# A gated linear-attention kernel with a fused MoE: the decay's row moved to the ACT queue and used one step later, another order of the first units, and the x transposes in another PSUM bank

## The chip, the cores and the metric

The kernel runs on one core of a Trainium2 chip. TensorE (PE) does matmuls and transposes, VectorE (DVE), ScalarE (ACT) and GpSimd (POOL) the elementwise work, and SyncE (SP) issues DMAs. An engine takes its instructions in order, so one that waits holds up all that stand behind it on that engine. The metric is device time in microseconds of one execution; several are made and the median is given. The profile comes from one more execution; its span runs from the first to the last instruction.

## The reference

Two stages are computed in float32. The first is a recurrence over 768 tokens for each of 4 batches and 8 heads of width 48, with a decay `w` per token and channel; the second is a two-matrix "maxout" MLP over the tokens.

```python
for t in range(S):                        # S = 768
    cur = einsum('bhd,bhe->bhde', u * kt, vt)
    y[:, :, t] = einsum('bhd,bhde->bhe', rt, state + cur)
    state = wt[:, :, :, None] * state + einsum('bhd,bhe->bhde', kt, vt)
x = y.transpose(0, 2, 1, 3).reshape(3072, 384)
out = maximum(x @ w1, x @ w2) @ w_out     # w1, w2: 384 x 1024, w_out: 1024 x 384
```

## The kernel before

The recurrence is done in chunks of 128 tokens. A **unit** is one chunk of two batches, so there are 12 units: unit n is chunk n // 2 of batches 0 and 1 (n even) or 2 and 3 (n odd). The 128 partitions hold 64 token pairs of each of the two batches. The state of the recurrence passes from unit n to unit n + 2, through `S_f` (float32) and `S_b` (bfloat16).

Each unit goes through three stages, and one **step** works on three units at once: stage A on unit n, stage T on unit n - 1, stage M on unit n - 2.

- Stage A: log of the decays (`logw`, done for the next unit), their prefix sum by a matmul with a triangular matrix (`cumsum`, into PSUM bank `ex`, line 195), exponentials (`exps`, lines 206 and 208), and the scaled r and k (`scale_rk`, lines 228 and 229). The sum of the whole chunk's logs, one row of `mz` per batch, is what the state decays by. It stands along one partition and is wanted down the partitions, so `exps` writes it to DRAM (`row`, line 212, two DMAs) and `decay_load` fetches it back into `WL` (line 221, two DMAs, element by element). Both are issued on SP.
- Stage T: transposes of the scaled r and k (`transp`, line 236, bank `tr`), the new state term (`kv`, into `T_f`), the scores (`scores`, lines 288 and 291), y (`y_inter`, `y_intra`), its cast to bfloat16 (line 328) and its transposes (`xt`, line 335, bank `tr` too, copied out by ACT at line 337). `decay_exp` (line 246, on ACT) turns `WL` into the decay factor, and `decay` (lines 274 and 277, on POOL) makes the next state of it, at the start of the following step.
- Stage M: the MLP. maximum(a, b) is taken as half of (a + b) + |a - b|: `gate` multiplies x by w1 - w2 and takes the absolute value (lines 347 and 351), `outp` adds the two products (lines 359 and 362), copies the result to `osb` (line 365) and stores it (line 368). The store's destination is seen as 2 x 64 x 384 (the two tokens of a pair, the pairs, the columns).

`weights` makes w1 - w2, w1 + w2 and the product (w1 + w2) w_out / 2 once (lines 142 to 156); it stands between stage T of unit 1 and the first stage M.

The order of work on every engine is the order in which it is written; no planner moves it. The three weights and the loads of units 0 to 2 are issued on SP ahead of all; in step n, SP gets the fetch of unit n - 1's decay, the eight load DMAs of unit n + 2 (line 77, 196,608 bytes each, w before k, r and v), unit n's row, and unit n - 2's two stores (196,608 bytes each). The load tiles have four buffers. Waits between engines are put in by the framework. It gives the DMAs, whichever queue they are on, eight completion counters in turn, and a DMA is issued only when the earlier one with its counter has landed.

Of the kernel before, what the change touches and what calls it, by code (L numbers as in the profile page):

```python
# [8 lines left out]
F32 = mybir.dt.float32  # L9
BF16 = mybir.dt.bfloat16  # L10
AF = mybir.ActivationFunctionType
# [23 lines left out]
def _body(tc, r, k, v, w, u, moe_w1, moe_w2, moe_w_out, out):  # L35
    nc = tc.nc
    B, H, S, D = r.shape
    P = 128
    C = 128
    Q = C // 2  # L40
    NC = S // C
    HD = H * D
    d_ff = moe_w1.shape[1]
    KO = HD // P
    FO = d_ff // P
    NP = H // 2
    DP = 64
    NU = NC * B // 2
# [15 lines left out]
    def unit(n):  # L64
        return n // 2, (n % 2) * 2
# [5 lines left out]
    def load(n):  # L71
        c, b0 = unit(n)
        d = {}
        for name, src in (("w", w), ("k", k), ("r", r), ("v", v)):
            t = ldp.tile([P, H, 2, D], F32, tag="l" + name, name="l" + name)
            for b in range(2):
                nc.sync.dma_start(  # L77
                    out=t[b * Q:(b + 1) * Q].rearrange("p h i d -> p h (i d)"),
                    in_=src[b0 + b, :, c * C:(c + 1) * C, :].rearrange(
                        "h (p i) d -> p h (i d)", i=2))  # L80
            d[name] = t
        L[n] = d
# [36 lines left out]
    for i in range(NRK):  # L119
        t = const.tile([P, 2, 2, H, DP], BF16, name=f"rkn{i}")  # L120
        nc.vector.memset(t, 0.0)
        rkn_b.append(t)

    S_f = [const.tile([P, 2, NP, D], F32, name=f"Sf{g}") for g in range(2)]
    T_f = [const.tile([P, 2, NP, D], F32, name=f"Tf{g}") for g in range(2)]
# [14 lines left out]
    def weights():  # L140
        for ko in range(KO):
            nc.vector.tensor_sub(wd_sb[:, ko, :], w1f[:, ko, :], w2f[:, ko, :])
            nc.vector.tensor_add(ws_sb[:, ko, :], w1f[:, ko, :], w2f[:, ko, :])
        nc.scalar.mul(wo_sb, wof, 0.5)
        for ko in range(KO):
            tp = pt_([P, FO, P], BF16, "tr")
            for fo in range(FO):
                nc.tensor.transpose(tp[:, fo, :], ws_sb[:, ko, fo * P:(fo + 1) * P], ident)
            nc.vector.tensor_copy(
                wsT_sb.rearrange("p f (k c) -> p k f c", k=KO)[:, ko, :, :], tp)  # L150
        for ko in range(KO):
            wc_p = pt_([P, HD], F32, "go", 2)
            for fo in range(FO):
                nc.tensor.matmul(wc_p, wsT_sb[:, fo, ko * P:(ko + 1) * P],  # L154
                                 wo_sb[:, fo, :], start=(fo == 0), stop=(fo == FO - 1))
            nc.scalar.copy(wc_sb[:, ko, :], wc_p)
# [7 lines left out]
    def logw(n):  # L164
        s = U[n] = {}
        s["lw"] = lw = wt_([P, H, 2, D], F32, "lw")
        nc.scalar.activation(lw, L[n]["w"], AF.Ln)  # L167
        s["lp"] = lp = wt_([P, H, D], F32, "lp")
        nc.gpsimd.tensor_add(lp, lw[:, :, 0, :], lw[:, :, 1, :])  # L169
# [21 lines left out]
    def cumsum(n):  # L191
        s = U[n]
        lw, lp = s["lw"], s["lp"]
        ex = pt_([P, HD], F32, "ex")
        nc.tensor.matmul(ex, tri2, lp.rearrange("p h d -> p (h d)"))  # L195
        s["A"] = A = wt_([P, 2, H, D], F32, "A")
        s["mz"] = mz = wt_([P, 2, HD], F32, "mz")
        exh = ex.rearrange("p (h d) -> p h d", h=H)
        nc.scalar.activation(A[:, 0], exh, AF.Exp)  # L199
        nc.vector.tensor_add(mz[:, 0].rearrange("p (h d) -> p h d", h=H), exh, lw[:, :, 0, :])  # L200
        nc.vector.tensor_add(mz[:, 1], ex, lp.rearrange("p h d -> p (h d)"))

    def exps(n):
        s = U[n]
        mz = s["mz"]
        nc.scalar.activation(s["A"][:, 1].rearrange("p h d -> p (h d)"), mz[:, 0], AF.Exp)
        s["iA"] = iA = wt_([P, 2, H, D], F32, "iA", 1)
        nc.scalar.activation(iA.rearrange("p i h d -> p i (h d)"), mz, AF.Exp, scale=-1.0)
        row = drp.tile([2, HD], F32, tag="row", name="row")
        for b in range(2):  # L210
            e = (b + 1) * Q
            nc.sync.dma_start(out=row[b:b + 1, :], in_=mz[e - 1:e, 1, :])
        s["row"] = row

    def decay_load(n):
        s = U[n]
        row = s["row"]
        s["WL"] = wl = WL[n % 2]
        rowv = row.rearrange("b (p r d) -> r d (b p)", r=2, d=D)
        for par in range(2):  # L220
            nc.sync.dma_start(
                out=wl[par * DP:par * DP + D, :, :].rearrange("d b p -> d (b p)"),
                in_=rowv[par])

    def scale_rk(n):
        s = U[n]
# [4 lines left out]
    def transp(n, x):  # L231
        s = U[n]
        tp = pt_([P, NP, 2, 2, Q], BF16, "tr")
        for i in range(2):
            for p in range(NP):
                nc.tensor.transpose(  # L236
                    tp[:, p, :, i, :],
                    s["rkn"][:, x, i, 2 * p:2 * p + 2, :].rearrange("s r d -> s (r d)"), ident)
# [4 lines left out]
    def decay_exp(n):  # L243
        s = U[n]
        s["Wt"] = wt = wt_([P, 2, NP, 1], F32, "Wt")
        nc.scalar.activation(wt.rearrange("p b q o -> p b (q o)"), s["WL"], AF.Exp)  # L246
# [82 lines left out]

    def xt(n):  # L330
        s = U[n]
        tp = pt_([P, KO, 2, P], BF16, "tr")
        for b in range(2):
            for ko in range(KO):
                nc.tensor.transpose(tp[:, ko, b, :], s["x"][:, b, ko * P:(ko + 1) * P], ident)  # L335
        s["xT"] = xT = wt_([P, KO, 2, P], BF16, "xT")
        nc.scalar.copy(xT, tp)  # L337
# [16 lines left out]
    def outp(n, b):  # L354
        c, b0 = unit(n)
        s = U[n]
        o = pt_([P, HD], F32, "go", 2)
        for ko in range(KO):
            nc.tensor.matmul(o, s["xT"][:, ko, b, :], wc_sb[:, ko, :],  # L359
                             start=(ko == 0), stop=False)  # L360
        for fo in range(FO):
            nc.tensor.matmul(o, s["gT"][:, fo, b, :], wo_sb[:, fo, :],  # L362
                             start=False, stop=(fo == FO - 1))
        osb = wt_([P, HD], F32, "osb", 6)
        nc.scalar.copy(osb, o)  # L365
        tok = (b0 + b) * S + c * C
        dst = out[tok:tok + C, :].rearrange("(q i) n -> i q n", i=2)
        nc.sync.dma_start(out=dst, in_=osb)


    def step(a, t, m):

        A, T, M = a is not None, t is not None, m is not None
        if T and t >= 1: decay(t - 1)
        if T: transp(t, 0)
        if A: cumsum(a)
        if M: gate(m, 0)
        if T: transp(t, 1)
        if A: exps(a)
        if A: bonus_mul(a)  # L380
        if M: gate(m, 1)
        if T: kv(t)
        if T: scores(t, 0)
        if A and a + 1 < NU: logw(a + 1)
        if M: gate(m, 2)
        if M: gate(m, 3)
        if T: decay_exp(t)
        if T: scores(t, 1)
        if T: y_inter(t)
        if A: scale_rk(a)  # L390
        if A: bonus_sum(a)
        if M: outp(m, 0)
        if T: y_intra(t)
        if M: outp(m, 1)
        if T: xt(t)
# [52 lines left out]
```

## Time and profile before

| | us |
|---|---|
| median of three runs | 240.19 (237.9 to 241.53) |
| the profiled execution | 237.25 |
| its span | 235.5 |
| PE busy | 157.3 (67%) |
| DVE busy | 106.7 (45%) |
| ACT busy | 91.2 (39%) |
| POOL busy | 105.7 (45%) |
| DMA engines (mean of 16) busy with the one hardware queue | 57.1% |

The page gives busy time of each engine, the chain of work that ended last (each piece followed back to what released it), and groups of instructions with what ended the idle time before them. A row of the chain reads: start, length, what. A row of the timeline reads: start, length, engine, line, operation, output <- inputs, count, and in brackets the idle time before it and what ended it. A row of waits reads: who waited for whom, then the total, the number and the longest of the waits. "SPq" is SP's queue: the time in which it issues a DMA. DMA share is the mean busy share of the core's 16 DMA engines; it can be above 1 where packets overlap.

### The profile page before, as it was taken

The numbers are of one execution on the slowest core, as the hardware profiler recorded it, in microseconds if no ns is written. First come the engines' busy times: TensorE is split into PE (matmuls) and PEld (weight loads), VectorE is DVE, ScalarE is ACT, GpSimd is POOL, SyncE is SP. The second block draws the span as 40 slices with busy tenths as digits, with TensorE's granted clock in tenths as the row PEclk, the third lists the DMA queues.
The fourth block names the chain that finished last, engine by engine and source line by source line (L and its number), as shares of the span: only waits on it lengthen the run. The fifth ranks groups of instructions, "written<-read, shape, count | busy, mean of one in ns | idle before, by whom it ended". The sixth has DMA issues, their size and how long they took to land.

```text
span 235.5 us, 5089 instructions
## 1 busy us (share of the span) xinstructions
PE 157.3 (67%) x2104; PEld 105.8 (45%) x2104; DVE 106.7 (45%) x135; ACT 91.2 (39%) x161; POOL 105.7 (45%) x116
## 2 busy tenths in 40 slices
PE   0316300553889979759889499893997939979820
PEld 0114200432555747437565375662665626665610
DVE  5336600189243837516666056570584905642000
ACT  3313001207164747047271463624536345453510
POOL 7299004910008759284393743947429476200000
PEclk9999999999999999968999779998599997999985
DMA  6999995959200386492674936939459201010110
GB/s 135 214 212 372 388 223 99 208 90 203 37 1 10 76 172 112 106 196 57 163 147 104 187 73 154 156 84 187 88 134 180 54 23 46 22 44 26 44 48 38
DMA packets 65463, 28.91 MB, mean 123 GB/s; under 512 B 60424, under 2 KB 64672, under 8 KB 65440
## 3 DMA queue, kind: packets, MB, share of 16 engines
q1 hardware_dynamic: 65440, 28.59, 57.1%
q8 instruction: 16, 0.26, 0.4%
q14 instruction: 7, 0.06, 0.1%
HBM read 23.83 MB, written 4.76 MB: 121 GB/s over the span
## 4 chain that ended last, share of the span: by engine, by line
PE 28%; DMA 21%; SPq 18%; DVE 12%; ACT 7%; issue 6%; POOL 3%; DVEq 0%; ACTq 0%
SPq L77 15%; DMA WL<-row 13%; DMA row<-mz 8%; PE go L347 6%; PE go L362 4%; PE tr L236 4%; PE ex L195 3%; ACT xT L337 2%; DVE M L291 2%; POOL vd L186 2%; PE go L154 2%; PE sc L288 2%; PE go L359 2%; DVE rkn L228 2%; PE tr L335 2%
## 5 line engine op out<-in xcount | busy, mean ns | idle before, releaser
L347 PE MATMUL go<-xT,wd_sb 128*128 128x256 bf16 x288 | 41.0, 290 | 2.0 <-ACT xT L337 0.9
L241 DVE COPY rT<-tr 128x1024 bf16<-128x1024 bf16 x12 | 8.3, 691 | 65.5 <-PE tr L236 65.5
L362 PE MATMUL go<-wo_sb,gT 128*128 128x384 bf16 x192 | 35.1, 326 | 0.0
L347 PEld LDWEIGHTS <-wd_sb 128*128 128x128 bf16 x288 | 28.8, 104 | 12.7 <-issue 7.1
L186 POOL TENSOR_TENSOR vd<-lv,dg 128x768 bf16<-128x768 f32 x12 | 17.7, 1474 | 36.9 <-DVE dg L184 36.8
L291 DVE TENSOR_TENSOR M<-sc,mask 128x1024 bf16<-128x1024 f32 x24 | 29.4, 1223 | 8.6 <-PE sc L288 8.6
L169 POOL TENSOR_TENSOR lp<-lw 128x384 f32<-128x384 f32 x12 | 12.0, 997 | 46.6 <-ACT lw L167 46.4
L351 ACT ACTIVATE gT<-go 128x512 bf16<-128x512 f32 x48 | 27.8, 593 | 9.7 <-PE go L347 9.2
L335 PE MATMUL tr<-ident,x 128*128 128x128 bf16 x72 | 7.3, 251 | 32.3 <-ACT x L328 32.3
L236 PE MATMUL tr<-ident,rkn 128*128 128x128 bf16 x192 | 19.3, 261 | 12.5 <-ACT xT L337 8.9
L246 ACT ACTIVATE Wt<-WL 128x8 f32<-128x8 f32 x12 | 2.5, 209 | 60.7 <-DMA WL<-row 60.7
L362 PEld LDWEIGHTS <-gT 128*128 128x128 bf16 x192 | 18.7, 98 | 12.5
L236 PEld LDWEIGHTS <-rkn 128*128 128x128 bf16 x192 | 16.6, 119 | 16.8 <-issue 12.0
L195 PE MATMUL ex<-lp,tri 128*128 128x384 f32 x24 | 14.8, 709 | 12.2 <-POOL lp L169 12.2
L176 POOL TENSOR_TENSOR rku<-lr,lk 128x768 f32<-128x768 f32 x12 | 22.4, 1866 | 0.0
L177 POOL TENSOR_TENSOR rku<-rku,u_b 128x768 f32<-128x768 f32 x12 | 21.8, 1815 | 0.9
L335 PEld LDWEIGHTS <-x 128*128 128x128 bf16 x72 | 5.1, 111 | 35.9 <-ACT x L328 35.6
L167 ACT ACTIVATE lw<-lw 128x768 f32<-128x768 f32 x12 | 10.0, 837 | 19.3 <-DMA lw<-in_w_dram 19.3
L359 PE MATMUL go<-wc_sb,xT 128*128 128x384 bf16 x72 | 15.7, 328 | 0.4 <-ACT gT L351 0.4
L200 DVE TENSOR_TENSOR mz<-ex,lw 128x384 f32<-128x384 f32 x12 | 6.7, 558 | 19.5 <-ACT A L199 19.5
L199 ACT ACTIVATE A<-ex 128x384 f32<-128x384 f32 x12 | 5.9, 490 | 23.9 <-PE ex L195 23.9
L365 ACT COPY osb<-go 128x384 f32<-128x384 f32 x24 | 11.4, 475 | 8.0 <-PE go L362 8.0
(55 smaller groups left out, 225.1 us busy)
## 6 DMA issues: line engine op xcount, KB each, us to landing
lw<-in_w_dram SPq DMA_DIRECT2D x24, 192.0 KB
lk<-in_k_dram SPq DMA_DIRECT2D x24, 192.0 KB
lr<-in_r_dram SPq DMA_DIRECT2D x24, 192.0 KB
lv<-in_v_dram SPq DMA_DIRECT2D x24, 192.0 KB
out_dram<-osb SPq DMA_DIRECT2D x24, 192.0 KB
w1f<-in_moe_w_dram SPq DMA_DIRECT2D x1, 1536.0 KB
w2f<-in_moe_w_dram SPq DMA_DIRECT2D x1, 1536.0 KB
wof<-in_moe_w_out_dram SPq DMA_DIRECT2D x1, 1536.0 KB
```

The costliest lines, as they stand in the source:

```text
L77: nc.sync.dma_start(out=t[b * Q:(b + 1) * Q].rearrange("p h i d -> p h (i d)"), in_=src[b0 + b, :, c * C:(c + 1) * C, :].rearrange("h (p i ...
L176: nc.gpsimd.tensor_mul(rku, L[n]["r"], L[n]["k"])
L177: nc.gpsimd.tensor_mul(byi(rku), byi(rku), u_b.rearrange("p (h d) -> p h d", h=H).unsqueeze(1).to_broadcast([P, 2, H, D]))
L186: nc.gpsimd.tensor_mul(byi_inv(vd), L[n]["v"], dg.to_broadcast([P, H, 2, D]))
L195: nc.tensor.matmul(ex, tri2, lp.rearrange("p h d -> p (h d)"))
L236: nc.tensor.transpose(tp[:, p, :, i, :], s["rkn"][:, x, i, 2 * p:2 * p + 2, :].rearrange("s r d -> s (r d)"), ident)
L291: nc.vector.tensor_mul(M.rearrange("s e p t -> s (e p) t"), sc.rearrange("s e p t -> s (e p) t"), mask[:, i].rearrange("s i q -> s (i q)") ...
L335: nc.tensor.transpose(tp[:, ko, b, :], s["x"][:, b, ko * P:(ko + 1) * P], ident)
L347: nc.tensor.matmul(g[:, f, :], wd_sb[:, ko, fo * P:(fo + 1) * P], s["xT"][:, ko].rearrange("p j t -> p (j t)"), start=(f == 0 and ko == 0) ...
L351: nc.scalar.activation(s["gT"][:, 2 * j:2 * j + 2].rearrange("p f j t -> p f (j t)"), g, AF.Abs)
L359: nc.tensor.matmul(o, s["xT"][:, ko, b, :], wc_sb[:, ko, :], start=(ko == 0), stop=False)
L362: nc.tensor.matmul(o, s["gT"][:, fo, b, :], wo_sb[:, fo, :], start=False, stop=(fo == FO - 1))
```

## The change

The diff does four things.

1. The chunk's row and its fetch are issued on ACT instead of SP. `mz` becomes two fixed tiles with the heads padded from 48 to 64 columns (cleared once by POOL), so the row is stored by one DMA and fetched by one DMA of 128 x 8 elements. The fetch stands at the start of stage T's step. For the last chunk (units 10 and 11), whose state nobody reads, row, fetch and exponential are left out.
2. `decay_exp` and `decay` of unit t - 1 stand in the middle of the step in which unit t is in stage T: the exponential comes one step after its fetch, and not in the same step.
3. The x transposes write bank `ex` instead of `tr`, and the output copies have four buffers instead of six.
4. The first steps are written out: in the step of unit 1 the log of unit 2 is left out; it is done after `weights`. The loads of units 3 and 4 stand after step 0 and after `weights`.

```diff
+    MZ = [const.tile([P, 2, H, DP], F32, name=f"mz{i}") for i in range(2)]
+    for t in MZ:
+        nc.gpsimd.memset(t, 0.0)
...
-        s["mz"] = mz = wt_([P, 2, HD], F32, "mz")
+        s["mz"] = mz = MZ[n % 2]
...
-        nc.vector.tensor_add(mz[:, 0].rearrange("p (h d) -> p h d", h=H), exh, lw[:, :, 0, :])
-        nc.vector.tensor_add(mz[:, 1], ex, lp.rearrange("p h d -> p (h d)"))
+        nc.vector.tensor_add(mz[:, 0, :, 0:D], exh, lw[:, :, 0, :])
+        nc.vector.tensor_add(mz[:, 1, :, 0:D], exh, lp)
...
-        row = drp.tile([2, HD], F32, tag="row", name="row")
-        for b in range(2):
-            e = (b + 1) * Q
-            nc.sync.dma_start(out=row[b:b + 1, :], in_=mz[e - 1:e, 1, :])
-        s["row"] = row
+        c, b0 = unit(n)
+        if c == NC - 1:
+            return
+        s["row"] = row = drp.tile([2, H * DP], F32, tag="row", name="row")
+        nc.scalar.dma_start(out=row, in_=mz[Q - 1::Q, 1].rearrange("b h d -> b (h d)"))

     def decay_load(n):
...
-        rowv = row.rearrange("b (p r d) -> r d (b p)", r=2, d=D)
-        for par in range(2):
-            nc.sync.dma_start(
-                out=wl[par * DP:par * DP + D, :, :].rearrange("d b p -> d (b p)"),
-                in_=rowv[par])
+        nc.scalar.dma_start(out=wl.rearrange("d b p -> d (b p)"),
+                            in_=s["row"].rearrange("b (p x) -> x (b p)", x=P))
...
     def xt(n):
         s = U[n]
-        tp = pt_([P, KO, 2, P], BF16, "tr")
+        tp = pt_([P, KO, 2, P], BF16, "ex")
...
-        osb = wt_([P, HD], F32, "osb", 6)
+        osb = wt_([P, HD], F32, "osb", 4)
...
-        if T and t >= 1: decay(t - 1)
+        if T: decay_load(t)
         if T: transp(t, 0)
...
         if T: scores(t, 0)
-        if A and a + 1 < NU: logw(a + 1)
+        if A and ahead and a + 1 < NU: logw(a + 1)
+        if T and t >= 1: decay_exp(t - 1)
+        if T and t >= 1: decay(t - 1)
         if M: gate(m, 2)
         if M: gate(m, 3)
-        if T: decay_exp(t)
         if T: scores(t, 1)
...
     logw(0)
-    for n in range(NU + 2):
-        a = n if n < NU else None
-        t = n - 1 if 0 <= n - 1 < NU else None
-        m = n - 2 if 0 <= n - 2 < NU else None
-        if t is not None:
-            decay_load(t)
-        if n >= 1 and n + 2 < NU:
-            load(n + 2)
-        if n == 2:
-            step(None, t, None)
-            weights()
-            step(a, None, m)
-        else:
-            step(a, t, m)
+    step(0, None, None)
+    load(3)
+    step(1, 0, None, ahead=False)
+    step(None, 1, None)
+    weights()
+    logw(2)
+    load(4)
+    step(2, None, 0)
+    for n in range(3, NU + 2):
+        if n + 2 < NU:
+            load(n + 2)
+        step(n if n < NU else None, n - 1 if n - 1 < NU else None, n - 2)
```

More of the change, by code (lines that the diff above doesn't have):

```diff
@@ L205, in exps @@
         mz = s["mz"]
-        nc.scalar.activation(s["A"][:, 1].rearrange("p h d -> p (h d)"), mz[:, 0], AF.Exp)
+        nc.scalar.activation(s["A"][:, 1], mz[:, 0, :, 0:D], AF.Exp)
         s["iA"] = iA = wt_([P, 2, H, D], F32, "iA", 1)
-        nc.scalar.activation(iA.rearrange("p i h d -> p i (h d)"), mz, AF.Exp, scale=-1.0)
-        row = drp.tile([2, HD], F32, tag="row", name="row")
-        for b in range(2):
-            e = (b + 1) * Q
-            nc.sync.dma_start(out=row[b:b + 1, :], in_=mz[e - 1:e, 1, :])
-        s["row"] = row
+        nc.scalar.activation(iA, mz[:, :, :, 0:D], AF.Exp, scale=-1.0)
+        c, b0 = unit(n)
[3 more added lines that the diff above has]
+        nc.scalar.dma_start(out=row, in_=mz[Q - 1::Q, 1].rearrange("b h d -> b (h d)"))
     def decay_load(n):
+        c, b0 = unit(n)
+        if c == NC - 1:
+            return
         s = U[n]
-        row = s["row"]
         s["WL"] = wl = WL[n % 2]
-        rowv = row.rearrange("b (p r d) -> r d (b p)", r=2, d=D)
-        for par in range(2):
-            nc.sync.dma_start(
-                out=wl[par * DP:par * DP + D, :, :].rearrange("d b p -> d (b p)"),
-                in_=rowv[par])
+        nc.scalar.dma_start(out=wl.rearrange("d b p -> d (b p)"),
+                            in_=s["row"].rearrange("b (p x) -> x (b p)", x=P))
     def scale_rk(n):
@@ L243, in decay_exp @@
     def decay_exp(n):
+        c, b0 = unit(n)
+        if c == NC - 1:
+            return
         s = U[n]
@@ L368, in outp, with step @@
         nc.sync.dma_start(out=dst, in_=osb)
-    def step(a, t, m):
+    def step(a, t, m, ahead=True):
         A, T, M = a is not None, t is not None, m is not None
-        if T and t >= 1: decay(t - 1)
+        if T: decay_load(t)
         if T: transp(t, 0)
```

## The prediction

> **What bounds the kernel now.** I read the page's chain, then the waits, then the stretches by step.
>
> ```profile
> span 235.5 us, 5089 instructions
> ...
> PE 28%; DMA 21%; SPq 18%; DVE 12%; ACT 7%; issue 6%; POOL 3%; DVEq 0%; ACTq 0%
> ...
> ACT Wt L246 <- DMA WL<-row: 60.7, 12, 9.9
> ACT lw L167 <- DMA lw<-in_w_dram: 19.3, 3, 13.7
> PE tr L236 <- ACT xT L337: 8.9, 10, 0.9
> ```
>
> ACT waits 60.7 us for the decay, and DMA and its issue are 39% of the chain. It is tempting to take the 60.7 us off. Before that, look at what the steps do when the wait varies. Here are three successive decay exponentials:
>
> ```profile
> 100.66 0.21 ACT L246 ACTIVATE Wt<-WL 128x8 f32<-128x8 f32 x1 [6.85 <-DMA WL<-row]
> 115.81 0.21 ACT L246 ACTIVATE Wt<-WL 128x8 f32<-128x8 f32 x1 [4.22 <-DMA WL<-row]
> 130.79 0.21 ACT L246 ACTIVATE Wt<-WL 128x8 f32<-128x8 f32 x1 [6.24 <-DMA WL<-row]
> ```
>
> They are 15.15 and 14.98 us apart, whether the wait is 4.22 or 6.24 us. The stretches (busy time of PE, PEld, DVE, ACT, POOL; clock; DMA share; GB/s) say the same, and say why:
>
> ```profile
> 42.50:48.50 6.00, 3.71 (x69) 2.92 (x68) 2.19 (x4) 0.80 (x1) 5.29 (x5) 1.00 1.30 202
> 219.00:225.00 6.00, 5.88 (x43) 3.91 (x41) 0.00 (x0) 2.87 (x5) 0.00 (x0) 1.00 0.13 48
> 103.70:118.54 14.84, 13.25 (x178) 8.97 (x178) 7.92 (x10) 7.00 (x13) 7.59 (x8) 0.85 0.62 133
> 118.54:133.84 15.30, 11.51 (x179) 7.83 (x179) 7.87 (x10) 6.90 (x13) 9.79 (x10) 0.94 0.64 133
> 182.00:183.00 1.00, 0.89 (x44) 0.66 (x33) 0.99 (x3) 1.00 (x3) 0.92 (x2) 1.00 0.14 45
> ```
>
> A step with PE at clock 0.85 and 13.25 us busy is no longer than one at 0.94 and 11.51: a step has some 2 to 4 us of room on PE, and something else sets 15 us. In 219 to 225 only output stores move: share 0.13, which is 2 of 16 engines, and 48 GB/s. A unit stores 2 x 196,608 bytes, so 393,216 / 48,000 = 8.19 us on those two. In 42.5 to 48.5 only a load moves, on all 16: 202 GB/s, so a unit's 8 x 196,608 bytes take 7.79 us. If the two engines of the stores also carry their sixteenth of each load, they have 8.19 + 7.79 = 16.0 us of work per step, against a period of 15.0. That they are always full explains the fixed period and this:
>
> ```profile
> 36.44 2.27 DMA row<-mz
> 39.13 2.00 DMA WL<-row
> 88.58 4.14 DMA row<-mz
> 93.16 7.39 DMA WL<-row
> ```
>
> The decay's 3 KB land in 2.00 us with no stores about and in 7.39 us behind them; the row's way to DRAM takes 2.27 and 4.14. So in steady state the decay wait is a symptom: take it away and ACT waits for loads queued on the same two engines.
>
> The Trainium skill, "DMA: Bandwidth & Descriptors", section "Why a DMA increments its semaphore by 16 and not by 1", has a rule that speaks against this change: a DMA from SP or ACT uses the largest number of engines up to 16 that divides the slowest dimension of both sides, and takes the lowest-numbered ones. The store's destination has a slowest dimension of 2 (the token pairs), so all stores would share two fixed engines, which the 0.13 bears out. That they are the same two each time no view here shows directly; the constant period agrees. By that rule the steady steps stay at 15; without it they would be those of rival (a), and the sum 199.
>
> **The change, part by part.** (1) The start. Unit 0 is ready for its x cast when its last y matmul ends, but ACT stands first at the log of unit 2, whose load queues behind 4.7 MB of weights, and then at the decay.
>
> ```profile
> 1.75 0.20 POOL L102 MEMSET tri<- 128x128 f32 x1
> 10.50 0.84 ACT L208 ACTIVATE iA<-mz 128x768 f32<-128x768 f32 x1
> 11.40 0.83 POOL L174 CAST vb<-lv 128x768 bf16<-128x768 f32 x1 [4.22 <-DMA lv<-in_v_dram]
> 17.59 1.65 PE L195 MATMUL ex<-lp,tri 128*128 128x384 f32 x2 [4.95 <-POOL lp L169]
> 19.28 0.49 ACT L199 ACTIVATE A<-ex 128x384 f32<-128x384 f32 x1 [4.61 <-PE ex L195]
> 25.42 0.50 PE L323 MATMUL y<-vb,M 64*128 64x48 bf16 x16 [0.25 <-DVE M L291]
> 35.44 0.84 ACT L167 ACTIVATE lw<-lw 128x768 f32<-128x768 f32 x1 [13.68 <-DMA lw<-in_w_dram]
> 36.36 0.99 POOL L169 TENSOR_TENSOR lp<-lw 128x384 f32<-128x384 f32 x1 [12.32 <-ACT lw L167]
> 41.33 0.78 ACT L328 CAST x<-y 128x768 bf16<-128x768 f32 x1
> 43.88 1.01 PE L236 MATMUL tr<-ident,rkn 128*128 128x128 bf16 x8 [0.89 <-ACT xT L337]
> 51.27 1.22 DVE L142 TENSOR_TENSOR wd_sb<-w1f,w2f 128x1024 bf16<-128x1024 f32 x1
> 66.51 0.81 PE L195 MATMUL ex<-lp,tri 128*128 128x384 f32 x2
> 66.71 0.48 ACT L156 CAST wc_sb<-go 128x384 bf16<-128x384 f32 x1 [0.82 <-PE go L154]
> 74.08 2.32 SPq L368 DMA_DIRECT2D out_dram<-osb  x2
> ```
>
> Afterwards neither wait stands there: x starts at 26.0 instead of 41.33 (15.3), and the next transposes need not wait 0.89 for the bank, as x now goes through the other one: 16.2 in all. The weights' DVE work moves from 51.27 to 35.1; w1 and w2 are queued ahead of the load that had landed by 35.44, so they are there, or late by tenths. All moves by 16.2 up to the last weight copy, 67.19 to 51.0. Now the log of unit 2 comes only here, and with it the pair sum: 0.84 + 0.99 and two hand-overs of 0.1, so the prefix matmul starts at 53.0 instead of 66.51: 13.5 stay. With the new row issue ahead of unit 0's last gates (0.4) the first store is issued at 61 instead of 74.08: **13 us gained**.
>
> (2) DMA issues on ACT. Per step one row store and one decay fetch.
>
> ```profile
> 35.94 0.73 SPq L212 DMA_DIRECT2D row<-mz  x2
> 38.76 0.84 SPq L221 DMA_DIRECT2D WL<-row  x2
> 92.78 1.47 SPq L221 DMA_DIRECT2D WL<-row  x2
> 16.87 6.45 SPq L77
> ```
>
> On SP an issue took 0.37 (row) and 0.42 to 0.74 us (fetch); the new fetch is one issue of 1024 elements instead of two of 384: between 0.42 (by issues) and 0.74 x 1024 / 384 = 2.0 (by elements). I take 0.4 + 1.0 per step, nearer the row without a backlog, as ACT's queue has none; the far end is the 6.45 that one load's issue was held up behind the weights. Behind the fetch on ACT stand A, every gate evacuation, and so PE. In the start the row is issued after iA at 11.3 and lands at 13.7 to 15.5 (2.27 to 4.14); A is due only at 19.28, so 3.8 us cover the fetch. In a steady step the cover is the wait for the prefix matmul and the 2 to 4 us of room; without cover it costs 1.4 us times seven.
>
> (3) The decay is used a step later: its exponential has more than a step to land, against 7.39 at worst, so the 60.7 us go. What is late next: the log's wait for a load.
>
> (4) Two clears on POOL of 1024 elements a partition. A 128-element one takes 0.20, so at most 8 x 0.20 = 1.6 each; PE waits 4.95 us at 17.59 for POOL's second unit, which itself waits for a load (4.22): nothing. Padded adds and exponentials process as many elements as before: nothing, or tenths. Four output buffers instead of six: a buffer is wanted two units later, when its store (queued ahead of a load that this step already needed) has landed: nothing. For the last two units no row, fetch, exponential: DMAs of 2 us, nothing.
>
> (5) Steady part. From the first store (74.08) to the end of the last load (182, from where the share is 0.14) the two engines do seven pairs of stores and seven loads: 107.9 us, 15.4 each. This stays: the last load ends at 61 + 108 = 169.
>
> (6) The tail. Five pairs of stores are left: 5 x 8.19 = 41; from 182 to 235.5 are 53.5, so 12.5 are idle now, since compute stands late.
>
> ```profile
> 122.75 0.83 ACT L167 ACTIVATE lw<-lw 128x768 f32<-128x768 f32 x1
> 118.54 0.61 PE L236 MATMUL tr<-ident,rkn 128*128 128x128 bf16 x8 [0.89 <-ACT xT L337]
> 127.87 1.47 PE L362 MATMUL go<-wo_sb,gT 128*128 128x384 bf16 x8
> 207.19 0.61 PE L236 MATMUL tr<-ident,rkn 128*128 128x128 bf16 x8 [0.93 <-ACT xT L337]
> 225.83 0.51 SPq L368 DMA_DIRECT2D out_dram<-osb  x1
> ```
>
> A step without decay wait is 129.34 - 118.54 = 10.8 plus the x transposes and their copy, about 12. The last log waits for the first quarter of the last load, 5.8 us before its end, and 8 us of that step follow (from 122.75 to 129.34, and the x transposes and copy); then one step of 12, the last two (207.19 to 225.83, 18.6) and the last store (225.83 to 235.5, 9.7): 2 to 8 us, plus 40.3, so 43 to 48 after the load. The two engines need 41 + 1.7. I take 45: **8.5 us gained**.
>
> Sum: span 235.5 - 13 - 8.5 = 214; outside the span lie 237.25 - 235.5 = 1.75, so 215.8 for an execution like the profiled one. The median shown, 240.19, is 1.2% above the profiled time, so 218 on its scale.
>
> **Rivals.** (a) *Steps run free.* If the two engines were no limit, nine steps of 12 follow 61, then 18.6 + 9.7 + 1.75: 199. For it: the 60.7 us. Against: the fixed period and 16.0 us of work. 5%.
>
> (b) *ACT is held in part.* The start's fetch comes late, behind the weights: x at 36 instead of 26 gives 226; or the period rises to 16.3, 228. For it: 6.45 for one issue. 17%. The same skill page, section "Queues, rings and completion order", says that each engine takes turns between the queues' rings, which would spare the fetch the stores ahead of it; all DMAs here sit on one queue, so no run here shows it, and by a single order the row would land like the 4.14 rather than the 2.27.
>
> (c) *Both*, and the gain is used up: about 237. 7%.
>
> (d) *Slower: ACT stops at its own row store.* DMAs of both queues share eight completion counters, and each waits until the earlier holder of its counter has landed. If the row store's holder is an early piece of the load just issued, ACT halts in mid-step until the preceding stores (8.19) and a quarter of the load (1.9) are through, counted from the previous step's end; 8.5 us of step follow: period 18.6. The load then ends at 61 + 7 x 18.6 = 191; 55 remain (that step's rest, two steps of 12, 28.3): 248. It decides from a period of 17.1, and shows as slower from 17.7. For it: ACT is in order and has no other place to wait. Against: the holder is the eighth DMA back, two thirds of a step old, mostly landed. 9%.
>
> **How the numbers follow.** The forecast (two engines bind, start and tail gained) has 62%, 211 to 224 alone. The range 206 to 236 takes in (b), half of (c) and the bounds of the start, leaving out (a), (d) and the rest of (c), some 2 in 10. Within 2% (235.4 to 245.0, about what this kernel's runs can tell from no change) lies (c): 7%; slower is (d): 9%; faster 84%.
>
> **What would show it.** The exponential's DMA wait is gone; a wait of the log (ACT) for the load appears from about the third full step, 2 to 6 us each; steps stay near 15 us with PE idle; the first store at 61, the last load done at 169. Stretches with only stores still show 0.13. Wrong would be: steps of 12 us (a), an ACT queue that waits at row or fetch (b, d), or x of unit 0 well after 26.

## The result, and the profile after

| us | before | after |
|---|---|---|
| median | 239.61 (237.9 to 241.53, four runs) | 227.98 (227.69 to 228.61, four runs) |
| the profiled execution | 237.25 | 228.61 |
| its span | 235.5 | 226.8 |

The four executions before are the three given above and one more. The ratio is 0.954, with a 95% interval of 0.948 to 0.960: the change makes the kernel faster by 4.6%. Every ratio in this document leaves out executions more than 1.5% slower than the fastest of the same kernel (one of the four before here, and three in the experiments). The prediction was 218.0, with a range of 206 to 236. The profiled executions differ by 8.7 us of span, where the prediction's sum had 21.5.

The page of the kernel after (span; chain of the work that ended last, by engine and by its first lines; the lines of code stand two to five numbers later than before):

```profile
span 226.8 us, 5085 instructions
...
DMA 20%; PE 16%; SPq 8%; ACT 5%; issue 2%; DVE 1%; POOL 0%; ACTq 0%; DVEq 0%
...
q10 hardware_dynamic: 10440, 0.08, 2.7%
```

This chain can be followed back only to 97.67 us and its shares add up to 52%, against 95% before, so the two can't be compared share by share. In its part of the span DMA leads, and all of its 20% is the log's load (`lw<-in_w_dram`); the decay's row and fetch, 21% of the span in the chain before, are gone from it. A second queue, ACT's (q10), carries the row and the fetch. The engines' waits in the same kernel (who for whom: total, number, longest):

```profile
ACT osb L370 <- PE go L367: 43.3, 24, 3.3
ACT lw L170 <- DMA lw<-in_w_dram: 29.2, 9, 5.6
PE go L364 <- ACT gT L356: 18.7, 7, 4.7
```

And the waits of SP's queue in it:

```profile
SPq L77 <- DMA WL<-row: 36.1, 9, 5.6
SPq L77 <- DMA row<-mz: 19.1, 2, 13.5
```

The 60.7 us that ACT waited for the decay are gone. Its log (line 170) now waits for loads instead, and a new wait has come that the prediction had not looked for: SP, which issues the loads and the stores, waits for the row and for the fetch that ACT issues.

The timeline of the kernel after, first the start on ACT, DVE and PE (start, length, what, and in brackets the idle time ahead of it):

```profile
26.44 0.80 ACT L333 CAST x<-y 128x768 bf16<-128x768 f32 x1 [4.20 <-PE y L328]
36.01 1.21 DVE L145 TENSOR_TENSOR wd_sb<-w1f,w2f 128x1024 bf16<-128x1024 f32 x1
52.72 0.48 ACT L159 CAST wc_sb<-go 128x384 bf16<-128x384 f32 x1 [0.82 <-PE go L157]
55.12 0.91 PE L198 MATMUL ex<-lp,tri 128*128 128x384 f32 x2 [2.44 <-POOL lp L172]
62.29 0.48 ACT L370 COPY osb<-go 128x384 f32<-128x384 f32 x1 [1.55 <-PE go L367]
```

The same timeline on SP's queue:

```profile
44.17 1.61 SPq L77 DMA_DIRECT2D lr<-in_r_dram  x2
59.34 1.27 SPq L77 DMA_DIRECT2D lv<-in_v_dram  x2
...
62.11 1.27 SPq L77 DMA_DIRECT2D lk<-in_k_dram  x2
69.04 1.28 SPq L77 DMA_DIRECT2D lr<-in_r_dram  x2
...
71.79 1.30 SPq L373 DMA_DIRECT2D out_dram<-osb  x2
...
178.85 38.62 SPq L373 DMA_DIRECT2D out_dram<-osb  x10
```

The compute is early, as predicted: the first output is copied by 62.77 (62.29 + 0.48). But its store leaves SP only at 71.79, hardly earlier than the 74.08 of before. SP stood still from 45.8 to 59.34 and from 63.4 to 69.04, with the store behind the loads of units 3 and 4. (The last row holds the pairs from the eighth on.) Then the steady part, by its logs on ACT:

```profile
115.80 0.84 ACT L170 ACTIVATE lw<-lw 128x768 f32<-128x768 f32 x1 [5.49 <-DMA lw<-in_w_dram]
130.55 0.84 ACT L170 ACTIVATE lw<-lw 128x768 f32<-128x768 f32 x1 [1.19 <-DMA lw<-in_w_dram]
147.13 0.84 ACT L170 ACTIVATE lw<-lw 128x768 f32<-128x768 f32 x1 [5.57 <-DMA lw<-in_w_dram]
```

They are 14.75 and 16.58 us apart, 15.7 on average, and each of them waits for its load, by turns 5 and 1 us. And the end, in the stretches of the same kernel (length, busy time of PE, PEld, DVE, ACT, POOL, then PE's clock, the DMA share and GB/s):

```profile
181.00:182.00 1.00, 1.00 (x5) 0.49 (x4) 0.00 (x0) 0.00 (x0) 0.88 (x3) 0.50 0.32 52
182.00:226.00 44.00, 31.60 (x389) 21.12 (x387) 11.18 (x13) 17.13 (x30) 9.02 (x8) 0.89 0.13 46
```

The last load is over by 182, as before, and from there only stores move, at a share of 0.13 and 46 GB/s. But what follows takes 44.8 us (226.8 - 182) instead of 53.5. So of the 8.7 us, 8.7 come from the tail; the 2.3 us by which the first store is earlier were used up on the way to the last load.

### The profile page after: what moved, and what is told of

It reads as the page before. It is cut to its first block, busy times and chain, and to the rows that moved or that the text cites. A ratio compares the mean times of both kernels' runs of the same rounds, so it can differ in the third digit from the quotient of the medians.

```text
span 226.8 us, 5085 instructions
## 1 busy us (share of the span) xinstructions
PE 159.0 (70%) x2104; PEld 104.3 (46%) x2104; DVE 114.1 (50%) x135; ACT 91.7 (40%) x159; POOL 113.6 (50%) x118
## 4 chain that ended last, share of the span: by engine, by line
DMA 20%; PE 16%; SPq 8%; ACT 5%; issue 2%; DVE 1%; POOL 0%; ACTq 0%; DVEq 0%
DMA lw<-in_w_dram 20%; PE go L367 6%; SPq L77 6%; PE go L352 3%; PE go L364 3%; SPq L373 2%; ACT gT L356 2%; PE sc L293 1%; PE y L328 1%; ACT xT L342 1%; ACT osb L370 1%; ACT lw L170 1%; DVE kT L243 1%; PE y L315 1%; PE y L308 1%
## 5 line engine op out<-in xcount | busy, mean ns | idle before, releaser
L367 PE MATMUL go<-wo_sb,gT 128*128 128x384 bf16 x192 | 40.8, 362 | 0.0
L352 PE MATMUL go<-xT,wd_sb 128*128 128x256 bf16 x288 | 37.2, 273 | 2.5 <-ACT xT L342 1.5
L364 PE MATMUL go<-wc_sb,xT 128*128 128x384 bf16 x72 | 19.0, 381 | 18.7 <-ACT gT L356 18.7
L243 DVE COPY rT<-tr 128x1024 bf16<-128x1024 bf16 x12 | 8.3, 688 | 45.8 <-PE tr L238 45.8
L198 PE MATMUL ex<-lp,tri 128*128 128x384 f32 x24 | 12.1, 592 | 19.5 <-POOL lp L172 14.8
L170 ACT ACTIVATE lw<-lw 128x768 f32<-128x768 f32 x12 | 10.1, 842 | 29.2 <-DMA lw<-in_w_dram 29.2
L238 PE MATMUL tr<-ident,rkn 128*128 128x128 bf16 x192 | 16.3, 234 | 4.3 <-DVE rkn L230 3.0
L364 PEld LDWEIGHTS <-xT 128*128 128x128 bf16 x72 | 6.5, 105 | 23.0 <-issue 21.0
L238 PEld LDWEIGHTS <-rkn 128*128 128x128 bf16 x192 | 13.6, 105 | 7.0 <-DVE rkn L230 4.4
L231 DVE TENSOR_TENSOR rkn<-lk,iA 128x768 bf16<-128x768 f32 x12 | 16.0, 1333 | 0.0
L230 DVE TENSOR_TENSOR rkn<-lr,A 128x768 bf16<-128x768 f32 x12 | 15.5, 1293 | 0.3 <-ACT A L209 0.2
L333 ACT CAST x<-y 128x768 bf16<-128x768 f32 x12 | 9.6, 798 | 13.1 <-PE y L328 12.9
```

What stands on the lines that cost most here:

```text
L230: nc.vector.tensor_mul(rkn[:, 0, :, :, 0:D], byi(L[n]["r"]), s["A"])
L231: nc.vector.tensor_mul(rkn[:, 1, :, :, 0:D], byi(L[n]["k"]), s["iA"])
L238: nc.tensor.transpose(tp[:, p, :, i, :], s["rkn"][:, x, i, 2 * p:2 * p + 2, :].rearrange("s r d -> s (r d)"), ident)
L352: nc.tensor.matmul(g[:, f, :], wd_sb[:, ko, fo * P:(fo + 1) * P], s["xT"][:, ko].rearrange("p j t -> p (j t)"), start=(f == 0 and ko == 0) ...
L364: nc.tensor.matmul(o, s["xT"][:, ko, b, :], wc_sb[:, ko, :], start=(ko == 0), stop=False)
L367: nc.tensor.matmul(o, s["gT"][:, fo, b, :], wo_sb[:, fo, :], start=False, stop=(fo == FO - 1))
```

## The experiments

Each was run beside the kernel before on the same chip; the ratio is to that one, with its 95% interval. "Unit 2's row" is the row and fetch of the decay of unit 2.

### What holds the first store: unit 2's row on SP

```diff
-        nc.scalar.dma_start(out=row, in_=mz[Q - 1::Q, 1]...)
+        (nc.sync if n == 2 else nc.scalar).dma_start(out=row, in_=mz[Q - 1::Q, 1]...)
...
-        nc.scalar.dma_start(out=wl.rearrange("d b p -> d (b p)"),
+        (nc.sync if n == 2 else nc.scalar).dma_start(out=wl.rearrange("d b p -> d (b p)"),
```

> The changed kernel, with only unit 2's row and fetch issued on SP again, so that no DMA of ACT's stands between the loads of units 3 and 4 in the order of the eight completion counters. Theory (SP is held: in the changed kernel the last loads of units 3 and 4 share a counter with ACT's row and fetch of unit 2 and wait for them, and the first store stands behind them on SP): the first store is issued at about 63 us instead of 71.8, the steady part (108 us) and the tail stay, and the time falls from 228 to 218 to 221. Rival (the first store waits because the engines of the stores are still busy with loads, or because it is computed late): the first store stays within 2 us of 72, time 226 to 229.

Measured: 216.08 us (214.94 to 216.3), ratio 0.897 (0.892 to 0.901). The first pair of stores in that kernel's timeline of SP:

```profile
62.25 2.30 SPq L373 DMA_DIRECT2D out_dram<-osb  x2
```

And what SP's queue waits for in it:

```profile
SPq L77 <- DMA WL<-row: 18.2, 5, 4.0
SPq L77 <- DMA row<-mz: 5.3, 1, 5.3
```

Moving two small DMAs of one unit to the other queue brings the first store from 71.79 to 62.25 and the time from 228.0 to 216.1. The wait of 13.5 us for a row is gone. The time is 2 us below what I expected, although the first store and the steady part came as forecast (62.25, and 109.8 us to the end of the last load at 172); the 2 us are the tail's, of which more below. How a load can wait for a row that it does not read is seen in the list of the kernel's instructions with the semaphores on which they wait (kernel after; DMAHW0 to 7 are the eight completion counters; `row_633` is unit 2's row, `lv_216` unit 3's v and `lr_609` unit 4's r):

```
SP   lv_216 <- in_v_dram        [waits DMAHW0]
SP   lr_609 <- in_r_dram        [waits DMAHW7]
ACT  WL0_168 <- row_633         [waits DMAHW7, DMAHW0, Activation]
```

The fetch of unit 2 (third row) waits for its row's landing on counter 0, so row_633 holds counter 0. The v load of unit 3 (first row) was given counter 0 next, eight DMAs later in the framework's count. But ACT comes to that row only at 57.73, after the exponentials of unit 2, and SP's load, ready at 45.8, has to stand until it has landed. The fetch then holds counter 7, and unit 4's r load waits for that until 69.04. The counters make the two queues one chain.

### What sets the steps: stores on 16 engines

In the kernel after, each store of 128 tokens is cut into its two halves, the even and the odd tokens of the pairs (64 partitions each), so that the slowest dimension of the destination is 64 and not 2. The bytes are the same.

```diff
-        nc.sync.dma_start(out=dst, in_=osb)
+        for i in range(2):
+            nc.sync.dma_start(out=dst[i], in_=osb[i * Q:(i + 1) * Q])
```

> The changed kernel, with each store cut in two of 64 rows, so that a store's slowest dimension is 64 and not 2. Theory (two engines carry all stores, and their queue sets the 15 us step): windows with stores show a share well above 0.13, a step falls to 12 to 13 us, bound by PE and ACT, and the time to 198 to 206. Rival (the loads as a whole, 1.97 MB a step over 16 engines, or the order of the counters set the step): the period stays at 15, time 225 to 230.

Measured: 201.52 us (200.52 to 206.09), ratio 0.836 (0.831 to 0.841). In its list of waits the log's wait for loads fell from 29.2 us to 12.6:

```profile
ACT lw L170 <- DMA lw<-in_w_dram: 12.6, 7, 3.3
```

while the first store is no earlier (70.82). That the cut stores run on more engines is seen late in this kernel, where the loads are over and nothing but a store moves:

```profile
196.50:197.00 0.50, 0.00 (x0) 0.00 (x0) 0.00 (x0) 0.00 (x0) 0.00 (x0) 1.00 0.60 141
```

The share is 0.60 and the rate 141 GB/s, where uncut stores alone show 0.13 and 46 to 51 GB/s. So 26 us of the kernel after went into stores that used two engines.

The same edit in the kernel before, nothing else:

> The kernel before, with the same cut of the stores and nothing else. Theory (the 60.7 us decay wait of ACT is a symptom of the two engines): row and fetch land in 2 to 4 us each, the decay wait falls below 25 us, the step to 12.5 to 13.5, time 208 to 218. Rival (the round trip through DRAM and its place on SP set the step themselves): the wait stays above 45 us, time 232 to 240.

Measured: 209.83 us (208.71 to 210.35), ratio 0.871 (0.866 to 0.876). Its wait for the decay, in the list of waits:

```profile
ACT Wt L246 <- DMA WL<-row: 15.4, 2, 10.0
```

Two successive decay exponentials in its timeline of ACT, which wait no more:

```profile
82.67 0.21 ACT L246 ACTIVATE Wt<-WL 128x8 f32<-128x8 f32 x1
94.73 0.21 ACT L246 ACTIVATE Wt<-WL 128x8 f32<-128x8 f32 x1
```

Of the 60.7 us of decay wait, 45 vanish (the 15.4 left are the two waits of the start) although the decay is fetched by the same DMAs, on the same queue, and used in the same step. The steps are 12.06 us apart instead of 15. The wait that led the list of the kernel before was a symptom of the stores.

### The parts of the change one by one

The later use of the decay alone, in the kernel before (rows and fetches stay on SP, old start, old bank):

```diff
-        if T and t >= 1: decay(t - 1)
         if T: transp(t, 0)
...
         if A and a + 1 < NU: logw(a + 1)
+        if T and t >= 1: decay_exp(t - 1)
+        if T and t >= 1: decay(t - 1)
         if M: gate(m, 2)
         if M: gate(m, 3)
-        if T: decay_exp(t)
```

> The kernel before, with only the exponential and the state update moved one step later; row and fetch stay on SP, old start. Theory (two engines bind the steady part): ACT's decay wait goes, the log's wait for its load takes its place, the step stays at 15; the start gains some 5 us (ACT leaves its first decay wait out) and the tail 8, time 225 to 230. Rival (a removed wait is time saved): a step of 12, time below 215.

Measured: 227.43 us (226.93 to 228.05), ratio 0.945 (0.940 to 0.950), as much as the whole change. Its two waits of ACT for DMAs, in the list of waits:

```profile
ACT lw L167 <- DMA lw<-in_w_dram: 36.2, 8, 13.9
ACT Wt L246 <- DMA WL<-row: 3.5, 2, 2.9
```

The new order of the first units alone, in the kernel before (fetch on SP ahead of the load, decay used in the same step):

```diff
-    for n in range(NU + 2):
-        ...
+    step(0, None, None)
+    decay_load(0)
+    load(3)
+    step(1, 0, None, ahead=False)
+    decay_load(1)
+    step(None, 1, None)
+    weights()
+    logw(2)
+    load(4)
+    step(2, None, 0)
+    for n in range(3, NU + 2):
+        ...
```

> The kernel before with only the new order of the first units (row and fetch on SP, the decay used in the same step, x transposes in their old bank, six output copies). My theory: the order alone leaves the decay wait of units 0 and 1 in ACT's queue ahead of their x casts, so x of unit 0 comes at 33 to 37 instead of 26; no ACT-issued DMA can hold SP, so the first store is issued at 64 to 70 instead of 74.1; steps stay at 15 and the tail stays at 53.5: 230 to 237 us. Rival, by which the start order is what the change gains from: 226 to 229. A second rival, that it is worth nothing without the other parts: 239 to 242.

Measured: 241.44 us (240.98 to 242.64), ratio 1.008 (1.005 to 1.010): nothing won, and my 230 to 237 was wrong, as was the first store, which leaves at 78.30 where I had 64 to 70. On ACT, in that kernel's timeline:

```profile
42.31 0.21 ACT L246 ACTIVATE Wt<-WL 128x8 f32<-128x8 f32 x1 [20.35 <-DMA WL<-row]
42.42 0.78 ACT L328 CAST x<-y 128x768 bf16<-128x768 f32 x1
```

And on SP's queue:

```profile
36.89 0.74 SPq L212 DMA_DIRECT2D row<-mz  x2
39.78 0.84 SPq L221 DMA_DIRECT2D WL<-row  x2
```

With the log taken away, the exponential of unit 0 stands first on ACT and waits the whole time, for a fetch that is not there; x comes at 42.42 instead of 41.33. I had expected 33 to 37; but row and fetch of unit 0 leave SP only at 36.89 and 39.78, behind the weights and the loads of unit 2.

The kernel after with the old loop in place of the new order:

> The kernel after with the loop's old order of the first units, the other parts kept. My theory: the start of the kernel after gains only 2.3 us on the one before (first store 71.8 against 74.1), the rest is the tail, which stays: 227 to 231 us, with the first store at 71 to 75. Rival, by which the new order is worth its predicted 13 us in some hidden way: 238 to 241.

Measured: 232.82 us (232.07 to 232.86), ratio 0.972 (0.969 to 0.974). That is 4.8 us slower than the kernel after, and just outside what I expected. On ACT, in its timeline, the log of unit 2 keeps the x cast of unit 0 until 39.67:

```profile
38.92 0.84 ACT L170 ACTIVATE lw<-lw 128x768 f32<-128x768 f32 x1 [16.85 <-DMA lw<-in_w_dram]
39.67 0.78 ACT L333 CAST x<-y 128x768 bf16<-128x768 f32 x1
```

So the new order gains 4.8 us together with the other parts of the change, and nothing alone in the kernel before (the run above). The kernel after with the old loop is also 5.4 us slower than the later decay alone (227.43), which differs from it by the ACT queue, the row's form in one DMA, the bank and the output copies: its first store leaves at 75.96, against 71.67 there. SP's queue shows the hold of ACT's row here too:

```profile
SPq L77 <- DMA row<-mz: 19.9, 2, 14.5
```

The 14.5 us end at 68.23, with the first store behind them, and the kernel with the later decay alone has no such wait of a load. The first output is copied by 71.7 in both kernels, so the hold accounts for the late first store; what the other parts add to the rest was not taken apart.

The kernel after with the x transposes back in their old bank (`"ex"` to `"tr"` in `xt`):

> The kernel after with the x transposes back in the bank of the r and k transposes. Then the next transposes wait some 0.9 us per step for ACT's copy, as they did before (8.9 us in ten waits). My theory: in the steady steps the two store engines set the pace and hide it; only in the start (once or twice) and in the last three steps it shows: 228 to 231 us. Rival, that PE's waits add up over the steps: 235 to 238. Rival, that the bank shared with the prefix sum costs as much as it saves: 227 to 228.5.

Measured: 227.90 us (224.97 to 230.1), ratio 0.942 (0.938 to 0.947). The median of all four is that of the new bank, and the ratio (from 224.97 and 226.40) is about 1% lower than the 0.954 with it: too little to call the old bank faster, but the new one gained nothing that shows. The waits say why: with the old bank the r and k transposes wait 9.3 us for ACT's copy in ten waits, and with the new one the prefix matmul waits for the same copy, 4.6 us in eight. My 228 to 231 was not met; the rival that the shared bank costs as much as it saves (227 to 228.5) was nearest.

### Which units want which queue

All rows and fetches on SP, the rest of the change kept:

```diff
-        nc.scalar.dma_start(out=row, in_=mz[Q - 1::Q, 1]...)
+        nc.sync.dma_start(out=row, in_=mz[Q - 1::Q, 1]...)
...
-        nc.scalar.dma_start(out=wl.rearrange("d b p -> d (b p)"),
+        nc.sync.dma_start(out=wl.rearrange("d b p -> d (b p)"),
```

> The kernel after with the row and the fetch of every unit issued on SP; the order of the first units, the later use of the decay, the bank of the x transposes and the four output copies stay. My theory: the hold-ups of SP by ACT's DMAs cost only where SP runs ahead of ACT, in the start; issued in SP's own order the rows hold nothing up, and the two engines of the stores set steps of 15: first store at 61 to 63, 214 to 218 us, as with unit 2 alone on SP. Rival, by which the fetch, now behind a load on SP, lands too late for its exponential, which would take the wait back to ACT: 222 to 230. Rival, that the ACT queue itself is worth something in the steady steps: 219 to 222.

Measured: 233.90 us (231.42 to 234.08), ratio 0.976 (0.970 to 0.981). My theory fell. The time is above all three of my ranges; the rival of the late fetch (222 to 230) came nearest, and it shows in two places. Two exponentials in its timeline of ACT:

```profile
49.15 0.21 ACT L251 ACTIVATE Wt<-WL 128x8 f32<-128x8 f32 x1 [20.21 <-DMA WL<-row]
104.13 0.21 ACT L251 ACTIVATE Wt<-WL 128x8 f32<-128x8 f32 x1 [4.20 <-DMA WL<-row]
```

In the start the exponential of unit 0 waits 20.21 us for a fetch that SP issues behind the weights and load 3, so x of unit 1 is late by 12.6 us (49.27 instead of 36.70) and the first store leaves at 70.34. And in the steps the exponential waits 3 to 5 us again, with pairs of stores 15.9 us apart. So the ACT queue seems worth its place for units 0 and 1, and costs for unit 2; the last run below tests the first half of this.

With the stores cut, the late fetch in the steps should not matter any more:

> As the previous kernel, with each store cut into two DMAs of 64 rows as well. If the remaining waits of SP in the version with unit 2 alone on SP and cut stores (196.7 us) came from ACT's rows, they go, and the log no longer waits for loads: 192 to 196 us. If they were hidden by PE's work (steps of 12 set by PE), the same 196 to 198 us. If the fetch behind the load comes late: over 199.

Measured: 201.61 us (201.49 to 202.03), ratio 0.841 (0.837 to 0.845), over 199 by the first place alone: its one wait for the decay, in the list of waits, is the start's.

```profile
ACT Wt L251 <- DMA WL<-row: 19.7, 1, 19.7
ACT lw L170 <- DMA lw<-in_w_dram: 5.5, 2, 3.5
```

After the start no log and no exponential waits for a DMA.

### Put together

Unit 2's row on SP and cut stores:

> The kernel after with both edits at once: row and fetch of unit 2 issued on SP, and each store cut into two DMAs of 64 rows. If the late first store and the two engines of the stores are two separate losses, they add: the first store at 62 instead of 71, and steps of 12 to 13.5 from there: 62 + (199.5 - 70.8) + 2 = 193, so 190 to 196 us. If the steps with spread stores are set by the loads alone, or if SP is held again and again by ACT's rows, the early start is lost by the end: 199 to 202 us, as with the cut stores alone.

Measured: 196.74 us (195.98 to 197.98), ratio 0.822 (0.818 to 0.826): just above the 190 to 196 that I expected. The two losses are separate ones, but do not add fully; SP is still held now and then by ACT's later rows, and three of the last four logs wait for their loads, up to 2.1 us.

Units 0 and 1 on ACT, all later ones on SP, and cut stores:

```diff
+        (nc.scalar if n < 2 else nc.sync).dma_start(out=row, in_=mz[Q - 1::Q, 1]...)
...
+        (nc.scalar if n < 2 else nc.sync).dma_start(out=wl.rearrange("d b p -> d (b p)"),
...
+        for i in range(2):
+            nc.sync.dma_start(out=dst[i], in_=osb[i * Q:(i + 1) * Q])
```

> The kernel after with row and fetch of units 0 and 1 on ACT, those of all later units on SP, and each store cut into two DMAs of 64 rows. My theory: the ACT queue is worth something only where SP stands behind the weights (units 0 and 1), and costs where it holds SP up (unit 2 on). So the early first store (62) comes together with the undisturbed steps (11.73 apart with all on SP): 62.2 + (199.7 - 70.6) + 2 = 193.3, so 192 to 195 us. Rival, that the last waits were hidden by the compute: 196 to 198, as with unit 2 alone on SP.

Measured: 192.70 us (192.19 to 192.97), ratio 0.802 (0.798 to 0.807): a fifth less than before, and 35 us less than the change as it was made. Three of its logs, in the timeline of ACT:

```profile
79.05 0.83 ACT L170 ACTIVATE lw<-lw 128x768 f32<-128x768 f32 x1
90.78 0.83 ACT L170 ACTIVATE lw<-lw 128x768 f32<-128x768 f32 x1
102.51 0.83 ACT L170 ACTIVATE lw<-lw 128x768 f32<-128x768 f32 x1
```

And what SP's queue waits for in it:

```profile
SPq L374 <- ACT osb L370: 37.8, 12, 8.1
SPq L77 <- DMA row<-mz: 5.4, 1, 5.4
SPq L77 <- DMA WL<-row: 4.2, 1, 4.2
```

The steps are 11.73 us apart and nothing in them waits for a load. The waits for a row and a fetch are those of the start, where units 0 and 1 use ACT; after it SP waits for the outputs, as a queue with nothing left to do should. The first store leaves at 61.94.

## Why the prediction was right, and where it was wrong

**The bound (right).** Two engines carry all stores, and their work, which I had estimated at 16.0 us for a period of 15.0, fixes the steps. Cutting the stores took 3 us off each step in the kernel before (15.0 to 12.06), and 2.6 in the one after (15.7 to 13.05 between logs, first to eighth), where SP is also held by ACT's rows. The rule of the Trainium skill on which this leaned ("DMA: Bandwidth & Descriptors", section "Why a DMA increments its semaphore by 16 and not by 1") is that a DMA uses as many engines as the largest number up to 16 that divides the slowest dimensions of both sides. The trace agrees: 64 in place of 2 is what was changed, the share of stores alone went from 0.13 to 0.60, and the log's and the exponential's waits fell with it. That it is the same two engines for every store is still only inferred. So the steps did not become 12 us by the change (rival (a), 199): that needs the store, which the change leaves as it is.

**The decay wait is a symptom (right).** 45 of its 60.7 us went without touching the decay, and in the kernel after it came back as the log's wait for loads, 29.2 us. I had forecast 2 to 6 us in each step from the third on; it was 5 in every second step and about 1 in those between.

**The start (failed).** The step that failed is "the first store is issued at 61 instead of 74.08: 13 us gained". Its compute half was right: x of unit 0 at 26.44 (predicted 26.0), the weights' DVE work at 36.01 (35.1), the last weight copy done at 53.2 (51.0), the prefix matmul at 55.12 (53.0), the output ready at 62.77; these are up to 2.2 us late, which left some 11 of the 13 us. What I left out is the queue between the output and its store. I had used the fact that all DMAs share eight counters only in rival (d), where ACT is held by SP's DMAs; I did not ask the reverse, whom a DMA on ACT holds, and the store stands on SP behind loads that were numbered after ACT's row. The term came out as 2.3 us instead of 13. With the hold removed (unit 2's row on SP) the first store left at 62.25, and the profiled execution took 214.9, against the 215.8 of my sum. That it comes so near is in part luck, since smaller errors cancel: the first store was 1.3 us later than 61, the steady part 1.9 longer than 107.9, and the tail 4 shorter than 45.

**The steady part (right, a little short).** From the first store to the end of the last load 107.9 us were carried over; it was 110 (182 - 71.79). The pairs of stores were 15.3 us apart ((178.85 - 71.79) / 7), against 15.4 forecast.

**The tail (right).** 44.8 us after the last load, forecast 45 (43 to 48), against 53.5 before: 8.7 us gained, forecast 8.5. In the profiled execution some 2 us of it were lost to a slow clock (below), an estimate: the work of PE from 179.43 to 184.7 took 5.2 us, and the same four groups of matmuls take 2.9 at the full clock from 193.51 on. With unit 2's row on SP the last load was over by 172, and 41 us followed (213.1 - 172), in which PE kept its full clock until its matmuls were done, as in this stretch of that kernel:

```profile
172.00:176.00 4.00, 3.42 (x38) 2.73 (x36) 1.56 (x3) 2.34 (x5) 3.92 (x4) 1.00 0.13 49
```

That is what the two engines need for the five pairs of stores alone (41 in my bound, to which I had added 1.7 without a row behind it). So the 44.8 met the forecast of 45 in part by luck: my sum had compute at the full clock, and without the slow clock the 44.8 would have been about 42.5, near the 41 of the stores.

**ACT's issues (mis-sized, without effect).** I took 0.4 + 1.0 us for row and fetch. In the trace of the kernel after (ACT's queue) they take

```profile
57.73 0.48 ACTq L216 DMA_DIRECT2D row<-mz  x1
64.17 0.36 ACTq L224 DMA_DIRECT2D WL<-row  x1
```

so 0.84 together (the very first row, at 11.59, took 1.02): the fetch of 1024 elements in one DMA costs by the issue, not by the element. The price of the fetch lies elsewhere: it was issued at 64.17, and the load that waits for its counter goes at 69.04, so it took up to 4.9 us to land, with loads under way but no store.

**The rivals.** The time, 228, is the one given for rival (b), "ACT is held in part", but not by its mechanism: ACT was held by its own DMAs neither at the start (x of unit 0 at 26.44) nor in the steps. Its sum was also off: a period of 16.3 gives 222 by the terms of my sum (61 + 7 x 16.3 + 45 + 1.75), 224 on the median's scale. Rival (d) named the right mechanism, the shared counters, and the wrong victim. So it was luck that 228 fell inside the range: it took the miss in only because its upper end had been drawn for another loss of the same size.

**The smaller edits (right).** POOL's two clears took 1.84 us together, where at most 1.6 each was predicted. The bank showed no gain. For the four output copies no run stands alone; SP's and ACT's lists of waits show none for them.

## What to carry to other kernels

Before a wait that leads the list is attacked, see whether the period changes when the wait does: if it doesn't, look for what is always full, and a DMA share of 2/16 in a stretch with one kind of transfer names it. A DMA moved to another queue is not independent of the first one as long as both draw their completion counters from one pool, as here: ask of each moved DMA not only whom it waits for, but which later DMA, on which queue, has to wait until it has been issued and has landed. A short DMA belongs on the queue that reaches it first: here ACT's for the units whose rows SP would issue only behind the weights, SP's for all that come later.

## What the runs showed that was not expected

**A wait costs clock as well.** In the kernel after PE stood still for 4.19 us at the last log that waited, and then ran at half its clock for about five. PE's timeline of that kernel:

```profile
179.43 1.12 PE L364 MATMUL go<-wc_sb,xT 128*128 128x384 bf16 x3 [4.19 <-ACT gT L356]
180.34 2.77 PE L367 MATMUL go<-wo_sb,gT 128*128 128x384 bf16 x8
184.51 1.46 PE L367 MATMUL go<-wo_sb,gT 128*128 128x384 bf16 x8
```

Three stretches of it, with PE's clock third from the end:

```profile
177.40:177.60 0.20, 0.00 (x0) 0.00 (x0) 0.20 (x1) 0.00 (x0) 0.00 (x0) 0.62 0.38 86
178.00:179.00 1.00, 0.00 (x0) 0.00 (x0) 0.23 (x1) 1.00 (x3) 0.13 (x1) 0.50 1.04 263
185.00:186.00 1.00, 1.00 (x10) 0.68 (x9) 0.00 (x0) 0.00 (x0) 1.00 (x1) 1.00 0.13 51
```

The same eight matmuls took 2.77 us at a clock of 0.50 and 1.46 at the full one. The Trainium skill, "TensorE: Matmul & The Clock Gate", section "Part 1: The HAM clock gate (the "warmup" mystery)", says that the clock is halved after an idle window of about 3.4 us and comes back after as long a busy one, in windows that run on freely. This stretch agrees in kind: the clock fell at about 177.4, within PE's 4.19 idle us, and was back by 185, some 5 us after PE had begun again. It does not agree in the length of the idle time: at 177.4 PE had been idle for 2.2 us (since 179.43 - 4.19 = 175.24), and in the three other long stalls of this kernel, which began at 82.22, 112.71 and 143.92, the clock fell 3.1, 3.3 and 2.8 us after PE's last matmul. The mean clock over the span fits as well: 0.933 in the kernel before and 0.921 after, 0.971 with unit 2's row on SP, and 0.997 in the fastest version, whose steps wait for nothing. So a part of the experiments' gains is PE's clock, which comes back when PE no longer stands still; how much, no run here separates. The change itself gained nothing by it.

**The ACT queue also held SP in the steps, and it cost little there.** In the kernel after SP waits 36.1 us for fetches in nine waits, and still the pairs of stores were 15.3 us apart, as in the version with the later decay alone, which has no DMA on ACT. A wait of SP counts only where SP is what the next transfer lacks: in the start, and again once the two engines of the stores no longer set the pace. With cut stores the logs stand 13.05 us apart with every row on ACT, 12.24 with unit 2's on SP, and 11.73 with those of units 0 and 1 alone on ACT.
